# An attention and two-MLP kernel ordered by a list scheduler: the first batch's averages handed to the MLP inside SBUF, and the scheduler's costs rewritten

## The chip, the cores and the metric

The kernel runs on one core of a Trainium2 chip. The metric is the device time of one execution in microseconds (us). Before the change three runs gave 923.7, 921.27 and 922.58; the median is 922.58.

## The reference

Causal attention with a bias from a cumulative sum, then two MLPs, all in fp32:

```python
B, H, S, D = 4, 8, 576, 64
scores = (q @ k.T) / 8
bias = -(cum[..., :, None] - cum[..., None, :])       # cum = cumsum(max(s, 0))
scores = where(causal, -1e9, scores + minimum(bias, 0))
attn = softmax(scores)
x = (attn @ v)            # to [2304 tokens, 512]
h = x @ w_in              # 512 -> 2048
x = (h * clip(h + 3, 0, 6) / 6) @ w_out               # 2048 -> 512
h = maximum(maximum(x @ w1, x @ w2), x @ w3)          # 512 -> 768
out = h @ w_out2          # 768 -> 512
```

Input weights come as 64-bit floats, and the kernel turns their bits into fp32 itself.

## The kernel before, in words

**Work.** Attention goes by batch b (0 to 3) and pair of heads p (0 to 3), two heads j each; a head has five chunks c of 128 queries, the last of 64. Below, (b,p,j) is a head and (b,p) a pair. Each chunk is a *slot* (`slot`): TensorE writes scores to `ps_s` (line 768; two cuts of 288 columns for the last chunk), VectorE adds the mask and takes the maximum (783), ScalarE takes the exponential into `e` (791), TensorE transposes to `pt` (813) and ScalarE drains that (354), from batch 1 on with VectorE's remainder (820). `average` multiplies with the values into `px` (844 for batch 0 in fp32; 852 for the others, high and low parts) and adds to the pair's tile `x32` (356, 354, 868). `finish` transposes the reciprocals of the sums to `pt_r` (908), multiplies `x32` with them (912), splits the result into `xs`, a rounded part (329 or 331) and a remainder on GpSimd (335), and stores it to DRAM, `x_d[b]` (one DMA of 576 KB for each pair). Then the pair is `stored`.

**Keys and queries.** `prepare` loads a pair's q and k (`qb`, `kb`), splits them into a rounded part and a remainder, and joins them by SBUF-to-SBUF DMAs into `qt` and `kt`: for each head one small row from `cum_d`, two of `qt<-qb` and three of `kt<-kb`. A head's scores wait for all six. All DMAs are issued by one queue, SP's (line 308).

**First MLP.** A unit u is 288 tokens, half a batch. `load_xs` waits until a batch's four pairs are stored and loads them from `x_d` into a tile `x` of a stock of two (four DMAs of 288 KB for a unit). `hidden1` multiplies (`ps_h`, 433 to 435: three matmuls for each of four chunks), `gate` forms `gt`, and `reduce1` multiplies again (`ps_x`). The tokens go through 6 of 16 blocks of the hidden dimension in a first pass (z = 0) beside attention, and through the other 10 in a second pass (z = 1), for which `x` is loaded from `x_d` again. The second MLP (`ps_j`, `ps_o`) follows. Weights come in 512 KB pieces (`raw`, two buffers) and are turned into fp32 by `bits_in`: ScalarE 386, VectorE 388, 394, 399 and 404, then a cast 329 or 331 and a subtraction on GpSimd in two halves (335). `w_in` has its first six pieces, and `w_out` too, early in the program.

**Order.** Nothing is ordered by hand. Each of these functions is a Python generator that asks for an engine and a cost (`yield "DVE", dve2(512)`) or waits for an event, and `Flow` plays it as a list scheduler in time order: of the requests that wait on a free engine the one of lowest rank is taken, and the instruction is issued there and then. So the costs (`mm`, `dve1`, `dve2`, `act1`, `pool1`, `pool2`) and the landing time of a DMA (`Flow.landing`) decide the order in which every engine's queue is written, and on the chip each engine takes its queue strictly in that order. The first MLP's matmuls have a rank behind all attention, so they fill what attention leaves. Before the change a DMA's landing is counted as

```python
self.dma = max(self.dma, self.cur.t + 0.65) + nbytes / 360e3
ev.set(at=self.dma + 0.9)
```

and VectorE and GpSimd never hinder each other.

Of the kernel before, what the change touches and what calls it, by code (L numbers as in the profile page):

```python
# [9 lines left out]
F32 = mybir.dt.float32  # L10
# [12 lines left out]
P = 128  # L23
# [84 lines left out]


class Flow:  # L110
    LATENCY = {"PE": 0.2, "DVE": 0.13, "ACT": 0.15, "POOL": 0.08, "SP": 0.0}

    def __init__(self):
        self.agenda, self.n, self.now = [], 0, 0.0
        self.free = {e: 0.0 for e in self.LATENCY}
        self.ready = {e: [] for e in self.LATENCY}
        self.dma = 0.0
        self.cur = None
        self.live = set()
# [52 lines left out]
    def dispatch(self, engine):  # L172
        while self.ready[engine] and self.free[engine] <= self.now + 1e-9:
            _, _, th, cost, chained, taken = heapq.heappop(self.ready[engine])
            if taken:
                continue
            taken.append(engine)
            self.free[engine] = self.now + cost
            later = 0.0 if chained else self.LATENCY[engine]
            th.t = self.now + cost + later  # L180
            self.at(self.free[engine], lambda: self.dispatch(engine), ORDER)
            self.step(th, engine)

    def landing(self, nbytes):
        ev = Event(self)
        self.dma = max(self.dma, self.cur.t + 0.65) + nbytes / 360e3
        ev.set(at=self.dma + 0.9)
        return ev
# [29 lines left out]
def pool1(n):  # L218
    return 0.161 + n / 1200.0


def pool2(n):
    return 0.148 + n * 0.0021

# [32 lines left out]
def attn_moe_moe2(ctx, tc, q, k, v, s, w_in, w_out, w1, w2, w3, w_out2, out):  # L257
# [59 lines left out]

    COST = {
        "copy": {"POOL": pool1, "ACT": act1, "DVE": dve1},
        "sub": {"POOL": pool2, "DVE": dve2},  # L320
        "bank": {"ACT": act2, "DVE": dve2},
# [52 lines left out]
    def bits_in(src, out):  # L374
# [11 lines left out]
        act.activation(m, hi.bitcast(F32), AF.Square)  # L386
        yield "DVE", dve2(512)
        vec.scalar_tensor_tensor(
# [3 lines left out]
        top = m.bitcast(U32)  # L392
        yield "DVE", dve1(512)
# [4 lines left out]
        yield "DVE", dve2(512)  # L398
# [4 lines left out]
        yield "DVE", dve2(512)  # L403
        vec.scalar_tensor_tensor(
# [137 lines left out]
    def cumulate():  # L542
# [8 lines left out]
        yield flow.landing(4 * B * H * S)  # L551
        yield "DVE", dve1(S)
        vec.tensor_scalar(out=sp_t, in0=sp_t, scalar1=0.0, scalar2=None, op0=ALU.max)
        yield "DVE", dve2(S)
# [4 lines left out]
        yield "DVE", dve1(S)  # L559
        vec.tensor_scalar(  # L560
# [21 lines left out]
    def load(dst, src, nbytes):  # L582
        yield DMA
        copy(dst, src)
        return flow.landing(nbytes)
# [161 lines left out]
    def slot(i, item, tiny):  # L747
# [11 lines left out]
        for lo, hi in cuts:  # L759
            bank = yield S_.get()  # L760
            ps = make(bank, [P, 512], F32, "ps_s")
            o = ps[:, 0:hi - lo]
            if (b, p) == (0, 0):
                yield "PE", len(passes) * 4 * mm(hi - lo), False, i - AHEAD
# [45 lines left out]
        pt = make(bank, [P, c + 1, n], F32, "pt")  # L810
        yield "PE", 2 * mm(n) * (c + 1)
        for y in range(c + 1):
# [13 lines left out]
    def average(b, p, j, g):  # L826
# [12 lines left out]
        for x in range(nj):  # L839
            last = x == nj - 1  # L840
            z = max(0, x * P - o)
            if b == 0:
                yield "PE", 4 * mm(n - z), not last
                pe.matmul(
# [49 lines left out]
    def finish(b, p):  # L894
# [4 lines left out]
        for g in range(2):  # L899
            _, o, n = GROUP[g]  # L900
            bank = yield T.get()
            ps = make(bank, [P, 512], F32, "pt_r")
            yield "PE", 2 * mm(n)
            for c in ((0, 1), (4, 2, 3))[g]:
# [9 lines left out]
            )  # L914
            T.put(bank)
        si = yield XS.get()
        xs = make(si, [P, 2, S], F32R, "xs")
# [15 lines left out]
    x_over, mp_over, x_closed = event(), event(), event()  # L933

    def load_xs():
        for z in range(2):
            for u in range(NU):
                b, o = divmod(u, 2)
                yield stored[b, 0]
                xi = yield X.get()  # L940
# [142 lines left out]
    def combined(dst, a, b_, op, n):  # L1083
        yield "DVE", dve2(n)
        vec.tensor_tensor(out=dst, in0=a, in1=b_, op=op)
# [206 lines left out]
    def join(dst, a, b_, op):  # L1292
        yield "DVE", dve2(U1)
        vec.tensor_tensor(out=dst, in0=a, in1=b_, op=op)
# [383 lines left out]
```

## Time and profile before

| | |
|---|---|
| median of three runs | 922.58 us |
| the profiled execution | 921.71 us |
| its span, first to last instruction | 919.9 us |
| instructions | 18687 |
| TensorE (PE) busy | 893.6 us, 97% |
| VectorE (DVE) busy | 711.5 us, 77% |
| ScalarE (ACT) busy | 478.6 us, 52% |
| GpSimd (POOL) busy | 193.6 us, 21% |
| mean granted TensorE clock | 0.990 |

Busy time is a share of the whole span. A matmul's end is modelled and overlaps the next one, so a "busy" PE may still wait for pieces shorter than that. Times inside the trace count from the first instruction. PE is the matrix engine, PEld its weight loads, SPq the queue that issues the DMAs.

### The profile page before, as it was taken

How to read it: one execution, taken by the hardware profiler on the slowest of the kernel's cores; microseconds unless marked ns; L12 is line 12 of the kernel's file. 1: busy time of each engine (PE TensorE's matmuls, PEld its weight loads, DVE VectorE, ACT ScalarE, POOL GpSimd, SP SyncE). 2: the span in 40 equal slices, each digit the busy share in tenths (PEclk: the TensorE clock that was granted, in tenths of full speed). 3: DMA queues.
4: the chain of work that ended last, by engine and by line, in shares of the span. 5: the costliest groups of instructions: out<-in, count | busy, mean ns of one | idle time of the engine just before them, and what ended most of it. 6: DMA issues, size and time to landing. Idle time of an engine off the chain costs nothing.

```text
span 919.9 us, 18687 instructions
## 1 busy us (share of the span) xinstructions
PE 893.6 (97%) x6532; PEld 862.6 (94%) x6532; DVE 711.5 (77%) x1818; ACT 478.6 (52%) x1216; POOL 193.6 (21%) x242
## 2 busy tenths in 40 slices
PE   9887899999999999999999999999999999999998
PEld 6666799999999999999999999999999999999998
DVE  6877988887888449997785989985758576777994
ACT  5775677787777545564453455454213142323452
POOL 5557855556543123300000000000000000000000
PEclk9998799999999999999999999999999999999999
DMA  7999877787785147665566697938842121283542
GB/s 222 225 267 269 231 210 204 201 245 211 204 204 152 50 158 215 211 193 163 164 221 246 192 340 259 355 143 311 285 145 72 59 66 43 91 288 109 166 140 78
DMA packets 97269, 174.93 MB, mean 190 GB/s; under 512 B 10620, under 2 KB 59772, under 8 KB 97176
## 3 DMA queue, kind: packets, MB, share of 16 engines
q1 hardware_dynamic: 97176, 173.75, 61.7%
q8 instruction: 52, 0.85, 0.4%
q14 instruction: 41, 0.34, 0.1%
HBM read 97.99 MB, written 49.17 MB: 160 GB/s over the span
## 4 chain that ended last, share of the span: by engine, by line
PE 84%; DVE 7%; DMA 6%; issue 2%; ACT 1%; SPq 1%; POOL 0%; DVEq 0%; POOLq 0%; ACTq 0%
PE ps_j L433 7%; PE ps_j L434 7%; PE ps_j L435 7%; PE ps_x L433 7%; PE ps_h L433 7%; PE ps_x L435 7%; PE ps_x L434 6%; PE ps_h L434 6%; PE ps_h L435 6%; PE ps_s L768 6%; PE px L852 4%; PE pt L813 4%; PE ps_o L434 2%; PE ps_o L435 2%; PE ps_o L433 2%
## 5 line engine op out<-in xcount | busy, mean ns | idle before, releaser
L433 PE MATMUL ps_h<-x,w 128*128 128x288 f32 x512 | 155.2, 303 | 0.0
L433 PE MATMUL ps_x<-gt,w 128*128 128x288 f32 x512 | 152.8, 298 | 0.3 <-DVE g L981 0.3
L435 PE MATMUL ps_x<-gt,w 128*128 128x288 f32 x512 | 151.1, 295 | 0.0
L434 PE MATMUL ps_h<-x,w 128*128 128x288 f32 x512 | 151.1, 295 | 0.0
L434 PE MATMUL ps_x<-gt,w 128*128 128x288 f32 x512 | 150.5, 294 | 0.3 <-DVE gt L335 0.3
L435 PE MATMUL ps_h<-x,w 128*128 128x288 f32 x512 | 150.7, 294 | 0.0
L434 PE MATMUL ps_j<-xf,wf 128*128 128x288 f32 x432 | 127.9, 296 | 0.0
L433 PE MATMUL ps_j<-xf,wf 128*128 128x288 f32 x432 | 127.7, 296 | 0.0
L435 PE MATMUL ps_j<-xf,wf 128*128 128x288 f32 x432 | 127.5, 295 | 0.0
L977 ACT ACTIVATE u<-ps_h,half 128x288 f32<-128x288 f32 x128 | 63.9, 499 | 97.8 <-PE ps_h L435 97.4
L791 ACT ACTIVATE e<-e,tiny 128x128 f32<-128x128 f32 (+4 forms) x160 | 95.9, 600 | 30.5 <-DVE tiny L783 29.6
L768 PE MATMUL ps_s<-kt,qt 128*128 128x288 f32 (+9 forms) x384 | 96.9, 349 | 8.7 <-DMA kt<-kb 4.3
L433 PEld LDWEIGHTS ps_h<-x,w 128*128 128x128 f32 x512 | 96.4, 188 | 1.0 <-DVE g L981 0.2
L433 PEld LDWEIGHTS ps_x<-gt,w 128*128 128x128 f32 x512 | 96.2, 188 | 0.9 <-DVE g L981 0.5
L434 PEld LDWEIGHTS ps_x<-gt,w 128*128 128x128 f32 x512 | 96.2, 188 | 0.8 <-DVE gt L335 0.6
L434 PEld LDWEIGHTS ps_h<-x,w 128*128 128x128 f32 x512 | 96.4, 188 | 0.1
L435 PEld LDWEIGHTS ps_h<-x,w 128*128 128x128 f32 x512 | 96.2, 188 | 0.0
L435 PEld LDWEIGHTS ps_x<-gt,w 128*128 128x128 f32 x512 | 96.2, 188 | 0.0
L783 DVE CUSTOM_DVE_ANT_0 e<-ps_s,above 128x128 f32<-128x128 f32 (+4 forms) x160 | 75.7, 478 | 21.5 <-PE ps_s L768 19.9
L981 DVE SCALAR_TENSOR_TENSOR g<-u,ps_h 128x288 f32<-128x288 f32 x128 | 57.6, 450 | 41.0 <-ACT u L977 39.9
L329 ACT ACTIVATE gt<-g 128x288 fp32r<-128x288 f32 x128 | 56.5, 441 | 50.0 <-DVE g L981 49.6
L434 PEld LDWEIGHTS ps_j<-xf,wf 128*128 128x128 f32 x432 | 81.4, 188 | 0.0
(157 smaller groups left out, 2112.7 us busy)
## 6 DMA issues: line engine op xcount, KB each, us to landing
x<-x_d SPq DMA_DIRECT2D x64, 288.0 KB
f_d<-wf SPq DMA_DIRECT2D x30, 512.0 KB
wf<-f_d SPq DMA_DIRECT2D x30, 512.0 KB
kt<-kb SPq DMA_DIRECT2D x90, 144.0 KB
raw<-in_w_out_dram SPq DMA_DIRECT2D x22, 512.0 KB
x_d<-xs SPq DMA_DIRECT2D x16, 576.0 KB
raw<-in_w_dram SPq DMA_DIRECT2D x18, 512.0 KB
qt<-qb SPq DMA_DIRECT2D x30, 288.0 KB
```

Source lines behind the costliest of these rows:

```text
L329: act.activation(dst, src, AF.Copy)
L433: pe.matmul(ps, lhsT=wh, rhs=xh, start=first, stop=False, skip_group_check=again)
L434: pe.matmul(ps, lhsT=wh, rhs=xl, start=False, stop=False, skip_group_check=again)
L435: pe.matmul(ps, lhsT=wl, rhs=xh, start=False, stop=last, skip_group_check=again)
L768: pe.matmul(o, lhsT=lhs[:, qs], rhs=rhs[:, lo:hi], start=(x == 0), stop=(x == len(passes) - 1),)
L783: vec.tensor_tensor_reduce(out=e[:, lo:hi], in0=ps[:, 0:hi - lo], in1=above[:, shift + lo:shift + hi], scale=-0.125, scalar=m0, op0=ALU.ad ...
L791: act.activation(e[:, :w], e[:, :w], AF.Exp, bias=m0, scale=-1.0, accum_out=r,)
L813: pe.transpose(pt[:, y, :], e[P - n:, y * P:(y + 1) * P], ident[P - n:, P - n:])
L852: pe.matmul(px[:, z:n], lhsT=vhl[:, x, j].rearrange("p l d -> p (l d)"), rhs=src[:, hl, x, z:n], start=(x + hl == 0), stop=(last and hl == 1),
L977: act.activation(ut, ps, AF.Relu, bias=half, scale=1.0 / 6.0)
L981: vec.scalar_tensor_tensor(out=g, in0=ut, scalar=1.0, in1=ps, op0=ALU.min, op1=ALU.mult)
```

## The change

Two things are done at once.

1. `finish` for batch 0 no longer uses `xs`. It takes both `x` tiles of the first MLP when pair (0,0) ends, and writes each pair's rounded part and remainder straight into them, by halves of 288 columns. After the fourth pair a unit's `x_ready` is set, and `load_xs` has nothing to load for units 0 and 1 in the first pass. The halves are still stored to `x_d` for the second pass, as eight DMAs of 288 KB out of `x`.
2. `Flow` counts otherwise. A matmul costs n/2245 + 0.004 (an fp32 one, all passes, n/600 + 0.01, a transpose n/1200 + 0.003). A DMA is counted by the length of its contiguous pieces, and slower from SBUF to SBUF. A cost of class `Held` (the GpSimd ones and VectorE's with operands in SBUF) takes a port that VectorE and GpSimd share, and starts only when that is free.

```diff
     def dispatch(self, engine):
...
+                if isinstance(one[3], Held) and self.port > self.now + 1e-9:
+                    passed.append(one)
+                else:
+                    chosen = one
...
     def landing(self, nbytes):
         ev = Event(self)
-        self.dma = max(self.dma, self.cur.t + 0.65) + nbytes / 360e3
-        ev.set(at=self.dma + 0.9)
+        took, after = self.moved
+        self.dma = max(self.dma, self.cur.t) + took
+        ev.set(at=self.dma + after)
         return ev
...
 def mm(n):
-    return n / 2400.0 + 0.003
+    return n / 2245.0 + 0.004
...
 def pool2(n):
-    return 0.148 + n * 0.0021
+    return Held(0.148 + n * 0.0021)
+def held2(n):
+    return Held(dve2(n))
...
     def copy(dst, src):
+        rows, r = src.ap[0][1], 4 if src.dtype != I64 else 8
+        nbytes = r
+        for _, n in src.ap:
+            nbytes *= n
+        r *= min(run_of(src), run_of(dst))
+        sides = [a.space == DRAM for a in (src, dst)]
+        if rows > 1:
+            r = min(r, nbytes // rows)
+        one = 0.010 if r <= 64 else 0.008 + r * 37.5e-6
+        if not any(sides):
+            one *= 1.6 if r < 3000 else 1.95
+        flow.moved = max(1.0, nbytes / r / 16.0) * one * 1.25, 1.5 if sides[0] else 0.9 if sides[1] else 1.0
...
     def finish(b, p):
...
+        if b == 0:
+            if p == 0:
+                for u in range(2):
+                    item = yield X.get()
+                    first_x[u].set((make(item, [P, 2, KD, U1], F32R, "x"), item))
+            for u in range(2):
+                x, item = yield first_x[u]
+                xc = x32[:, u * U1:(u + 1) * U1]
+                yield from rounded(x[:, 0, p], xc, U1, ON["xh"])
+                yield from minus(x[:, 1, p], xc, x[:, 0, p].bitcast(F32), U1, ON["xl"])
+                first_count[u] += 1
+                if first_count[u] == NPAIR:
+                    x_ready[0, u].set((x, item))
+            X32.put(xi)
+            for u in range(2):
+                x, item = yield first_x[u]
+                d = yield from load(
+                    x_d[0][:, p, :, u * U1:(u + 1) * U1].rearrange("l p t -> p l t"),
+                    x[:, :, p], 8 * P * U1,
+                )
+            yield d
+            stored[0, p].set()
+            finished[0] += 1
+            return
...
     def load_xs():
...
+                if (z, b) == (0, 0):
+                    yield x_ready[z, u]
+                    continue
```

Because of the second part the order changes on every engine, and three places show it. Line numbers after the change are 59 higher in this part of the code (768 is 827, 813 is 872, 844 is 903, 852 is 911, 908 is 967, 783 is 842, 912 is 971).

PE before, where pair (0,3) ends. `vhl` marks averages of batch 1:

```order
L768 MATMUL ps_s<-kt,qt 128x256 x2
L908 MATMUL pt_r<-ident,ex 128x128 x2
L813 MATMUL pt<-ident,e_188 128x64 x5
L813 MATMUL pt<-ident,e 128x128
L768 MATMUL ps_s<-kt,qt 128x384 x2
L908 MATMUL pt_r<-ident,ex 128x128 x3
L813 MATMUL pt<-ident,e 128x128 x2
L852 MATMUL px<-e_1185,vhl 128x320 x2
```

PE after, the same place, up to the first `ps_h` (492):

```order
L903 MATMUL px<-e2p,vf_745 128x320 x3
L903 MATMUL px<-e2p,vf_745 128x192
L903 MATMUL px<-e2p,vf_745 128x64
L967 MATMUL pt_r<-ident,ex 128x128 x5
L827 MATMUL ps_s<-kt,qt 128x128 x2
L827 MATMUL ps_s<-kt,qt 128x256 x2
L872 MATMUL pt<-ident,e 128x128
L827 MATMUL ps_s<-kt,qt 128x384 x2
L872 MATMUL pt<-ident,e 128x128 x2
L492 MATMUL ps_h<-x,w 128x288
```

Before, 70 PE instructions lie between the last `pt_r` of pair (0,3) and the first `ps_h`; now 9 do. Ahead of the first `ps_h` stood 130 `ps_s`, 160 `pt` and 84 `px`; now 96, 123 and 56. The 99 that went are batch 1's and come behind it; in front of it, batch 0's last three heads now have PE to themselves, one after the other.

SP before, the store of pair (0,3) and what follows up to the last loads of unit 0 and the first of unit 1:

```order
L308 DMA x_d_58<-xs 128x2x576
L308 DMA qt<-qb 64x1152
L308 DMA kt<-kb 64x576
L308 DMA x<-x_d_58 128x2x288
L308 DMA kt<-cum_d 2x576
L308 DMA qt<-qb 64x576
L308 DMA kt<-kb 64x576 x2
L308 DMA qt<-qb 64x1152
L308 DMA kt<-kb 64x576
L308 DMA x<-x_d_58 128x2x288 x4
```

All eight loads `x<-x_d` of units 0 and 1 are gone after the change.

SP after, where the last head of batch 0, (0,3,1), is joined:

```order
L367 DMA kt<-cum_d 2x576
L367 DMA vf<-in_v_dram 128x640
L367 DMA qt<-qb 64x576
L367 DMA kt<-kb 64x576
L367 DMA x_d_58<-x 128x2x288
L367 DMA kt<-kb 64x576
L367 DMA x_d_58<-x 128x2x288
L367 DMA qt<-qb 64x1152
L367 DMA kt<-kb 64x576
L367 DMA raw<-in_w_out_dram 128x512 x2
L367 DMA x_d_58<-x 128x2x288 x2
```

The two single stores are pair (0,1)'s. The store of that pair came six rows behind the last join of (0,3,1) before; now it stands among these joins. The sizes of all DMAs up to that last join add up to 15.2 MB before and 15.0 MB after, in 66 and 67 DMAs.

DVE after, behind the last maximum of (0,3,1), from the third instruction to the last multiplication of batch 0 (`dm`, `da` and `w` turn a piece of `w_out` into fp32, `x_905` is the pair's `x32`):

```order
L453 TENSOR_SCALAR da<-dm 128x512
L939 TENSOR_SCALAR sums<-sums 128x10
L458 SCALAR_TENSOR_TENSOR da<-dm,da 128x512
L941 RECIPROCAL sums<-sums 128x10
L463 SCALAR_TENSOR_TENSOR da<-raw,da 128x512
L447 SCALAR_TENSOR_TENSOR dm<-dm,raw 128x512
L390 CAST w<-da 128x512
L453 TENSOR_SCALAR da<-dm 128x512
L458 SCALAR_TENSOR_TENSOR da<-dm,da 128x512
L971 TENSOR_TENSOR x_905<-x_905,pt_r 128x256
L463 SCALAR_TENSOR_TENSOR da<-raw,da 128x512
L971 TENSOR_TENSOR x_905<-x_905,pt_r 128x320
```

With a `dm` (447) and a copy of `px` (415) ahead of these, fourteen instructions lie between the last maximum and the end of the pair. Before, batch 1's maxima and remainders stood in this stretch as well; they have moved behind it.

## Rows read from the trace of the kernel before

**Rows 1.** Stretches: length, busy us (instructions) by engine, granted clock, DMA share, GB/s.

```profile
0.00:113.00 113.00, 93.73 (x508) 73.98 (x509) 89.55 (x245) 73.44 (x198) 71.60 (x91) 0.92 0.92 244
113.00:460.00 347.00, 345.01 (x2611) 335.40 (x2611) 272.67 (x727) 225.63 (x575) 121.97 (x152) 1.00 0.65 185
460.00:920.00 460.00, 454.89 (x3416) 453.18 (x3415) 349.29 (x849) 179.48 (x444) 0.00 (x0) 1.00 0.53 180
```

**Rows 2.** Timeline of PE: start, length, what, [idle before, who ended it].

```profile
66.93 0.71 PE L768 MATMUL ps_s<-kt,qt 128*128 128x128 f32 x4 [0.95 <-DMA kt<-kb]
...
80.99 0.52 PE L813 MATMUL pt<-ident,e 64*128 64x64 f32 x5 [2.90 <-ACT e L791]
83.11 1.65 PE L844 MATMUL px<-e1p,vf 128*128 128x256 f32 x4 [1.59 <-DVE x L356]
...
113.01 0.34 PE L433 MATMUL ps_h<-x,w 128*128 128x288 f32 x1
```

**Rows 3.** Shorter stretches, columns as in rows 1.

```profile
23.00:46.00 23.00, 18.74 (x113) 14.27 (x112) 20.53 (x50) 16.57 (x44) 13.59 (x16) 1.00 1.00 225
46.00:69.00 23.00, 18.87 (x119) 15.47 (x119) 16.69 (x58) 17.27 (x50) 11.84 (x16) 1.00 1.03 267
...
161.00:184.00 23.00, 23.00 (x175) 21.93 (x174) 18.51 (x58) 17.27 (x51) 13.07 (x18) 1.00 0.76 201
```

**Rows 4.** Timeline of SP, the queue that issues the DMAs.

```profile
13.73 5.08 SPq L308 DMA_DIRECT2D raw<-in_w_in_dram  x2
...
60.43 0.60 SPq L308 DMA_DIRECT2D kt<-kb  x1
...
66.18 0.53 SPq L308 DMA_DIRECT2D x_d<-xs  x1
...
102.49 0.53 SPq L308 DMA_DIRECT2D x_d<-xs  x1
...
112.20 3.18 SPq L308 DMA_DIRECT2D x<-x_d  x4
```

**Rows 5.** Timeline, the end of pair (0,3).

```profile
96.27 0.49 DVE L912 TENSOR_TENSOR x<-x,pt_r 128x320 f32<-128x320 f32 x1
96.97 0.67 ACT L329 ACTIVATE xs<-x 128x576 fp32r<-128x576 f32 x1
...
100.27 1.25 POOL L335 TENSOR_TENSOR xs<-x,xs 128x288 fp32r<-128x288 f32 x1
```

**Rows 6.** The chain that ended last, 60 to 114 us: start, length, what.

```profile
71.08 8.43 DMA raw<-in_w_out_dram
79.52 0.67 ACT dm L386
```

**Rows 7.** Groups of the page: busy us, mean ns | idle before.

```profile
L783 DVE CUSTOM_DVE_ANT_0 e<-ps_s,above 128x128 f32<-128x128 f32 (+4 forms) x160 | 75.7, 478 | 21.5 <-PE ps_s L768 19.9
```

**Rows 8.** Groups of DVE in 0 to 113 us, by form.

```profile
L404 DVE SCALAR_TENSOR_TENSOR da<-raw,da 128x512 uint32<-128x512 uint32 x11 | 10.3, 936 | 0.1
L388 DVE SCALAR_TENSOR_TENSOR dm<-dm,raw 128x512 f32<-128x512 f32 x12 | 10.1, 838 | 4.7 <-ACT dm L386 4.7
L399 DVE SCALAR_TENSOR_TENSOR da<-dm,da 128x512 uint32<-128x512 uint32 x11 | 9.8, 891 | 0.2
...
L394 DVE TENSOR_SCALAR da<-dm 128x512 uint32<-128x512 uint32 x11 | 5.6, 513 | 0.1
```

**Rows 9.** The same for POOL.

```profile
L335 POOL TENSOR_TENSOR xs<-x,xs 128x288 fp32r<-128x288 f32 x8 | 7.3, 916 | 0.8 <-DVE xs L331 0.4 <-DVE sums L880 0.4
```

**Rows 10.** Timeline of POOL, pair (0,1)'s last remainder.

```profile
63.17 0.99 POOL L335 TENSOR_TENSOR xs<-x,xs 128x288 fp32r<-128x288 f32 x1
```

**Rows 11.** Stretches, columns as in rows 1.

```profile
78.00:82.00 4.00, 0.62 (x6) 0.39 (x5) 1.79 (x5) 1.93 (x5) 4.00 (x6) 1.00 1.07 294
82.00:86.00 4.00, 2.89 (x10) 2.71 (x11) 3.93 (x7) 2.15 (x6) 4.00 (x5) 0.55 1.06 237
86.00:90.00 4.00, 4.00 (x13) 2.84 (x12) 2.87 (x11) 1.97 (x5) 2.18 (x3) 0.60 1.01 339
```

More of the change, by code (lines that the diff above doesn't have):

```diff
@@ L107, in rank @@
         return self.prio
+class Held(float):
+    pass
 class Flow:
@@ L117, in __init__ @@
         self.dma = 0.0
+        self.port = 0.0
         self.cur = None
@@ L172, in dispatch @@
     def dispatch(self, engine):
[L173 to L176, printed above, removed]
+        ready = self.ready[engine]
+        while ready and self.free[engine] <= self.now + 1e-9:
+            passed, chosen = [], None
+            while ready and chosen is None:
+                one = heapq.heappop(ready)
+                if one[5]:
+                    continue
[3 more added lines that the diff above has]
+                    chosen = one
+            for one in passed:
+                heapq.heappush(ready, one)
+            if chosen is None:
+                return
+            _, _, th, cost, chained, taken = chosen
             taken.append(engine)
             self.free[engine] = self.now + cost
+            if isinstance(cost, Held):
+                self.port = self.now + cost
+                for other in ("DVE", "POOL"):
+                    if other != engine:
+                        self.at(self.port, lambda other=other: self.dispatch(other), ORDER)
             later = 0.0 if chained else self.LATENCY[engine]
@@ L198, in mm, with mm4, mmt @@
 def mm(n):
-    return n / 2400.0 + 0.003
+    return n / 2245.0 + 0.004
+def mm4(n):
+    return n / 600.0 + 0.01
+def mmt(n):
+    return n / 1200.0 + 0.003
 def dve1(n):
@@ L218, in pool1, with held1 @@
 def pool1(n):
-    return 0.161 + n / 1200.0
+    return Held(0.161 + n / 1200.0)
 def pool2(n):
-    return 0.148 + n * 0.0021
+    return Held(0.148 + n * 0.0021)
+def held1(n):
+    return Held(dve1(n))
+def held2(n):
+    return Held(dve2(n))
 DMA = ("SP", 0.45)
@@ L305, in stack, with run_of @@
         return [(pl, f"{tag}{x}") for x in range(n)]
-    def copy(dst, src):
+    def run_of(a):
+        r = 1
+        for step, n in reversed(a.ap):
+            if step != r:
+                break
+            r *= n
+        return r
+    def copy(dst, src):
+        rows, r = src.ap[0][1], 4 if src.dtype != I64 else 8
[10 more added lines that the diff above has]
+        flow.moved = max(1.0, nbytes / r / 16.0) * one * 1.25, 1.5 if sides[0] else 0.9 if sides[1] else 1.0
         sp.dma_start(
@@ L318, in attn_moe_moe2 @@
     COST = {
-        "copy": {"POOL": pool1, "ACT": act1, "DVE": dve1},
-        "sub": {"POOL": pool2, "DVE": dve2},
+        "copy": {"POOL": pool1, "ACT": act1, "DVE": held1},
+        "sub": {"POOL": pool2, "DVE": held2},
         "bank": {"ACT": act2, "DVE": dve2},
@@ L386, in bits_in @@
         act.activation(m, hi.bitcast(F32), AF.Square)
-        yield "DVE", dve2(512)
+        yield "DVE", held2(512)
         vec.scalar_tensor_tensor(
@@ L392, in bits_in @@
         top = m.bitcast(U32)
-        yield "DVE", dve1(512)
+        yield "DVE", held1(512)
         vec.tensor_scalar(
@@ L397, in bits_in @@
         )
-        yield "DVE", dve2(512)
+        yield "DVE", held2(512)
         vec.scalar_tensor_tensor(
@@ L402, in bits_in @@
         )
-        yield "DVE", dve2(512)
+        yield "DVE", held2(512)
         vec.scalar_tensor_tensor(
@@ L551, in cumulate @@
         yield flow.landing(4 * B * H * S)
-        yield "DVE", dve1(S)
+        yield "DVE", held1(S)
         vec.tensor_scalar(out=sp_t, in0=sp_t, scalar1=0.0, scalar2=None, op0=ALU.max)
-        yield "DVE", dve2(S)
+        yield "DVE", held2(S)
         vec.tensor_tensor_scan(
@@ L558, in cumulate @@
         QHL.put(a)
-        yield "DVE", dve1(S)
+        yield "DVE", held1(S)
         vec.tensor_scalar(
@@ L763, in slot @@
             if (b, p) == (0, 0):
-                yield "PE", len(passes) * 4 * mm(hi - lo), False, i - AHEAD
+                yield "PE", len(passes) * mm4(hi - lo), False, i - AHEAD
             else:
@@ L810, in slot @@
         pt = make(bank, [P, c + 1, n], F32, "pt")
-        yield "PE", 2 * mm(n) * (c + 1)
+        yield "PE", mmt(n) * (c + 1)
         for y in range(c + 1):
@@ L842, in average @@
             if b == 0:
-                yield "PE", 4 * mm(n - z), not last
+                yield "PE", mm4(n - z), not last
                 pe.matmul(
@@ L902, in finish @@
             ps = make(bank, [P, 512], F32, "pt_r")
-            yield "PE", 2 * mm(n)
+            yield "PE", mmt(n)
             for c in ((0, 1), (4, 2, 3))[g]:
@@ L915, in finish @@
             T.put(bank)
+        if b == 0:
[21 more added lines that the diff above has]
+            finished[0] += 1
+            return
         si = yield XS.get()
@@ L933, in attn_moe_moe2 @@
     x_over, mp_over, x_closed = event(), event(), event()
+    first_x, first_count = [event(), event()], [0, 0]
     def load_xs():
@@ L938, in load_xs @@
                 b, o = divmod(u, 2)
+                if (z, b) == (0, 0):
+                    yield x_ready[z, u]
+                    continue
                 yield stored[b, 0]
@@ L1083, in combined @@
     def combined(dst, a, b_, op, n):
-        yield "DVE", dve2(n)
+        yield "DVE", held2(n)
         vec.tensor_tensor(out=dst, in0=a, in1=b_, op=op)
@@ L1292, in join @@
     def join(dst, a, b_, op):
-        yield "DVE", dve2(U1)
+        yield "DVE", held2(U1)
         vec.tensor_tensor(out=dst, in0=a, in1=b_, op=op)
```

## The prediction, as it was put on record

> **What bounds the kernel now.** I read the busy time by stretches first. From 113 us on, PE is busy 345.01 of 347.00 us and then 454.89 of 460.00; in the first 113 us only 93.73 of 113.00, at a mean granted clock of 0.92 [rows 1]. So behind 113 us the kernel is bound by PE's work, and what can be won there is the 7 us of idle time. Ahead of it some 20 us are idle, and part of the rest runs at the lower clock. 113 us is no chance place: it is when the first `ps_h` starts [rows 2], the MLP's matmul that fills what attention leaves open. Since all PE work behind it lies almost without a gap, the time of the kernel is the moment of the first `ps_h` plus the PE work that the order puts behind it. The prediction is these two numbers.
>
> The shorter stretches tell what bounds the part ahead. From 23 to 69 us the DMA share is 1.00 and 1.03 while PE is busy 18.7 of 23 us [rows 3]: the joins of keys and queries are late. In PE's timeline the scores of the last head of batch 0, (0,3,1), start at 66.93, ended by DMA `kt<-kb` [rows 2]. Its own last join was issued at 60.43 [rows 4], 6.5 us earlier. From there to the first `ps_h` 46 us pass, and two things fill them. First, the pair ends late: `x32` is multiplied last at 96.27 [rows 5], after waits of PE of 2.90 us for the exponential and 1.59 us for a copy [rows 2]. The chain of waits puts these down to a piece of `w_out` that was on its way for 8.43 us, from 71.08, and to the decoding behind it [rows 6]: ScalarE and VectorE stood in their queues at a piece that the scheduler had thought landed. Second, the trip through DRAM: the remainder ends at 101.5 [rows 5], the store is issued at 102.49, the last loads of the unit at 112.20 [rows 4], and the matmul starts at 113.01. From the last multiplication that is 16.3 us.
>
> **The change, part by part.** *The trip through DRAM* goes: unit 0 is ready when the last remainder is written. Eight loads of 288 KB leave SP's queue; four stores of 576 KB become eight of 288 KB, off the path, since only the second pass reads them. Four casts of 576 columns become eight of 288: one of 576 took 0.67 [rows 5], so less than 0.67 more for each pair beside other work; I cost it at nothing but for the last one, which is on the path.
>
> *The order.* 99 PE instructions of batch 1 move behind the first `ps_h`. In a dense stretch of attention and MLP together 175 instructions take 23.00 us [rows 3], 0.131 each, so the work behind grows by 99 x 0.131 = 13.0 us. The part behind was 919.9 - 113.0 = 806.9 us, and becomes 819.9. This is what the change has to pay: if the first `ps_h` came no earlier than 100.0, nothing would be won.
>
> *When the first `ps_h` comes.* The DMAs up to the last join of (0,3,1) are 15.0 MB where they were 15.2. While the DMA engines are full that is the same moment, so the scores of that head start at 66.9 again. From there I add up the path by the new order, in which PE and VectorE do little but this head:
>
> - the first scores 0.71 [rows 2], six maxima at 0.478 each [rows 7], 2.9: 70.5;
> - the fourteen instructions of VectorE up to the last multiplication. Eight are the decoding: two each of 0.838, 0.513, 0.891 and 0.936 [rows 8], 6.4. The other six (a copy, two on the sums, a cast, two multiplications) at the 0.49 of the multiplication [rows 5], 2.9. Together 9.3: 79.8;
> - the cast, at most 0.67 [rows 5], and GpSimd's remainder, 0.92 [rows 9]: 81.4.
>
> Exponentials, transposes and averages of that head run on other engines beside these fourteen. If the decoding were not there they would be the path, so it is no sum of both.
>
> Two things may delay this. The stores of pair (0,1) now stand among the joins of (0,3,1), and SP waits for what it is to store: behind them in SP's queue are the last `qt` and `kt` of that head, and PE's scores wait for those. Before, the last remainder of that pair ended at 63.17 + 0.99 = 64.2 [rows 10] and the store was issued at 66.18 [rows 4]; were it as late now, the joins would move by 66.2 - 60.4 = 5.8 us. At best they move by nothing, since 12 fewer score instructions stand ahead of that pair's end. And the granted clock may fall: in 82 to 90 us, behind a stretch in which PE was busy 0.62 of 4 us, it was 0.55 and 0.60 [rows 11], where about half of the 6.9 busy us, 3.4, was lost. So between 0 and 9.2 us; I take 3.6, nearer to the low end, because part of a late join is covered (its DMAs then find the engines less full) and because the old stall of PE had a cause that the new order takes away. On the other side, SP stood 5.08 us at two pieces of `w_in` at 13.73 [rows 4]; one of them is issued later now, and if the joins come earlier by the 4 us or so of that wait, the path ends at 77.4.
>
> So the first `ps_h` comes at 85.0 (77.4 to 90.6). Sum: 819.9 + 85.0 = 904.9 us of span. The profiled execution is 921.71 for a span of 919.9, and the median of the runs 922.58, so 2.7 go on top: **907.6 us** (900 to 913 for this case alone).
>
> *Behind the first `ps_h`* I change nothing. The filler must last: units 0 and 1 have 288 matmuls in the first pass, 288 x 0.131 = 37.7 us, and the order spreads them to beyond the end of batch 1 as before. In the second pass and the second MLP PE's order is nearly the same. VectorE's and ScalarE's shares of casts change hands there; that work lies beside 450 of 460 us of PE.
>
> *The costs themselves* are no instructions; their whole effect is the order.
>
> **Rivals.** *The end of batch 0 stays where it was* (no change). VectorE is busy 89.55 of 113 us [rows 1], and if it and the DMAs, not the order, set the pair's end, the multiplication ends at 96.27 + 0.49 again; with 0.67 and 0.92 the first `ps_h` comes at 98.4, and the time is 819.9 + 98.4 + 2.7 = 921.0. The 16.3 us of the trip are then nearly all paid back by the work that moved. For it speaks that the order still puts two decodings into the tail, whose pieces may land late. Against it: VectorE has nine maxima, with their reads, and all of batch 1's remainders less to do ahead of that point.
>
> *The clock falls for the last heads* (slower). From (0,2,1) on each head of batch 0 now has PE alone, in the order score, transpose, average, with nothing of batch 1 between; 121 PE instructions lie from there to the first `ps_h`. In 46 to 69 us 119 took 18.87 us at full clock [rows 3]; at half, 121 would take 19.2 more. With none of it hidden the first `ps_h` comes at 104.2, and the time is 926.8. It decides once 17.7 of the 19.2 us are lost. Against it: the clock held at 1.00 through 23 to 69 us though PE was idle for a fifth of it [rows 3]. The Trainium skill's page "TensorE: Matmul & The Clock Gate" (Part 1) speaks for it: it calls the half rate the default, released only by activity. By that rule a thinner stretch of PE is the place to lose the clock, and the time would be this rival's; the trace agrees in the stretch behind 78 us and not in the one before.
>
> **How the numbers follow.** About 0.3%, 2.8 us, is what a measurement of this kernel can tell from no change: faster is below 919.8, slower above 925.3. The forecast has 0.79; the end of batch 0 unmoved 0.13, which counts as the same; the clock 0.08, slower. The range holds the forecast's own bounds, with 1 us below for joins that come earlier still, and reaches up to the first rival: 899 to 921. It leaves out the clock and a little of either side.
>
> **What would show it.** The first `ps_h` at 77 to 91 us; no `x<-x_d` for units 0 and 1; the first scores of (0,3,1) near 67 us, without a piece of `w_out` holding ScalarE for several us behind them; PE dense from the first `ps_h` on. Wrong would be: the first `ps_h` at 96 or later; a clock near 0.5 between 60 us and it; SP standing at a store `x_d<-x` ahead of the last joins by more than 6 us; or new gaps of PE behind it, where batch 1's scores wait for their joins or unit 2 for its loads, each of which adds its own length.

## The result, and the profile after

The changed kernel takes 913.19 us (median; 912.86 to 913.57) against 923.14 for the kernel before in the same session: ratio 0.9888, 95% interval 0.9874 to 0.9901. The profiled execution has a span of 911.8 us, 8.1 less than before. The forecast was 907.6, so two thirds of the forecast gain of 15 us came; the result lies inside the range of 899 to 921.

The three stretches of [rows 1], of the kernel after (columns as there):

```profile
0.00:113.00 113.00, 101.40 (x608) 81.60 (x609) 86.96 (x256) 78.67 (x213) 63.72 (x86) 0.98 0.86 225
113.00:460.00 347.00, 342.63 (x2559) 331.25 (x2559) 273.82 (x728) 225.60 (x577) 127.35 (x160) 0.99 0.67 188
460.00:912.00 452.00, 447.58 (x3369) 446.81 (x3367) 342.10 (x836) 174.22 (x430) 0.00 (x0) 1.00 0.54 181
```

By 113 us PE has done 608 instructions where it had done 508: a lead of 100. The next 347 us hold only 2559 where they held 2611: 52 of the 100 are lost again. Shorter stretches show where:

```profile
92.00:115.00 23.00, 22.03 (x166) 20.63 (x166) 21.51 (x61) 18.41 (x52) 17.04 (x21) 1.00 0.79 186
115.00:138.00 23.00, 19.55 (x123) 16.94 (x123) 20.29 (x58) 14.14 (x39) 17.20 (x22) 0.90 0.82 205
138.00:161.00 23.00, 23.00 (x167) 21.93 (x167) 17.54 (x60) 16.66 (x48) 12.92 (x18) 0.95 0.65 181
```

From 115 to 138 us PE does 123 instructions, 52 fewer than in a dense stretch [rows 3]. PE's timeline has the last head of batch 0, the first `ps_h` and the new gap:

```profile
69.44 2.38 PE L903 MATMUL px<-e2p,vf 128*128 128x320 f32 x10 [0.53 <-ACT e2p L413]
71.62 1.06 PE L827 MATMUL ps_s<-kt,qt 128*128 128x128 f32 x6
...
78.69 4.06 PE L903 MATMUL px<-e2p,vf 128*128 128x320 f32 x10 [0.53 <-ACT e2p L413]
82.59 0.72 PE L967 MATMUL pt_r<-ident,ex 128*128 128x128 f32 x5
...
86.04 0.38 PE L492 MATMUL ps_h<-x,w 128*128 128x288 f32 x1
...
123.47 0.29 PE L494 MATMUL ps_x<-gt,w 128*128 128x288 f32 x1
...
124.26 0.29 PE L494 MATMUL ps_h<-x,w 128*128 128x288 f32 x1
...
138.94 0.49 PE L492 MATMUL ps_x<-gt,w 128*128 128x288 f32 x1
```

The end of the pair, which answers to [rows 5], takes 1.6 us where the trip through DRAM took 16.3:

```profile
83.01 0.42 DVE L971 TENSOR_TENSOR x<-x,pt_r 128x256 f32<-128x256 f32 x1 [1.17 <-PE pt_r L967]
...
83.95 0.48 DVE L971 TENSOR_TENSOR x<-x,pt_r 128x320 f32<-128x320 f32 x1
...
84.47 0.44 ACT L388 ACTIVATE x<-x 128x288 fp32r<-128x288 f32 x1 [1.25 <-DVE x L971]
...
84.99 1.00 POOL L394 TENSOR_TENSOR x<-x,x 128x288 fp32r<-128x288 f32 x1 [2.56 <-ACT x L388]
```

The first `ps_h` starts at 86.04. Between 123.47 and 138.94 there is no `ps_x`, and behind the one at 124.26 no `ps_h` either: all nine `gt` tiles are full, and the next `ps_x` needs the sixth piece of `w_out`. Its decoding lies thinly in VectorE's queue, and ends with GpSimd's subtraction:

```profile
124.26 0.77 DVE L447 SCALAR_TENSOR_TENSOR dm<-dm,raw 128x512 f32<-128x512 f32 x1
...
127.48 0.63 DVE L453 TENSOR_SCALAR da<-dm 128x512 uint32<-128x512 uint32 x1
...
132.93 0.99 DVE L458 SCALAR_TENSOR_TENSOR da<-dm,da 128x512 uint32<-128x512 uint32 x1
...
134.05 0.68 DVE L463 SCALAR_TENSOR_TENSOR da<-raw,da 128x512 uint32<-128x512 uint32 x1
...
135.79 0.41 DVE L390 CAST w<-da 128x512 fp32r<-128x512 f32 x1
...
138.27 0.72 POOL L394 TENSOR_TENSOR w<-da,w 128x256 fp32r<-128x256 f32 x1
```

Before, that subtraction stood at 120.81:

```profile
120.81 0.95 POOL L335 TENSOR_TENSOR w<-da,w 128x256 fp32r<-128x256 f32 x1
```

**An account of PE's time.** For every kind and shape of PE instruction I took the lower quartile of the time from its start to the next start (median over the kernels) as its dense pace, and call what a kernel takes beyond that its *loss*. All fourteen kernels run the same 6532 PE instructions, so span minus loss is the same in all by construction (845.2 to 845.7 us): the table tells where time is lost, not why. It is of one execution each, and executions of one kernel differ: the changed kernel's by 0.7 us, those of the kernel before lay between 917.65 and 928.88, and e4's profiled one, at 930.59, is among its slowest. So a difference of a microsecond or two in a cell says little. In us, by stretch; "first" and "145th" are `ps_h`, the 145th being the first of batch 1; "left" is how many of the first pass's 864 matmuls are not yet done when attention's last `pt_r` starts. The names are those of the experiments below.

```
          0-84 84-113 113-140 140-230 230-345 345-460 460-end  loss  span  first 145th last pt_r left
before    27.5  13.8    3.0     8.2     9.0     2.4    10.4    74.3 919.9 113.0 193.9  326.8   192
after     25.9   2.7   10.6     8.5     8.2     2.0     8.5    66.4 911.8  86.0 197.2  321.1   192
e1        25.0  10.5    6.3     8.9    10.7    15.8     9.7    86.9 932.2  94.9 195.1  345.0    54
e2        24.9  18.0    7.8     8.6     8.7     1.9     9.1    79.0 924.2 126.7 213.9  324.5   258
e3        25.6   5.4    2.4    13.7     9.9    16.5    11.1    84.6 930.3  87.0 199.7  340.5    54
e4        28.3   7.1    8.0    11.8     9.1     6.3    13.0    83.6 928.8 100.7 195.1  338.8   123
e6        25.0   8.0    2.7    14.0     8.3     8.4    10.9    77.3 922.6  89.1 202.1  323.3   192
e7        23.3  11.8    7.2     8.8     9.2     3.5    11.8    75.6 920.9  92.3 195.5  327.7   177
e8        24.2   8.7    4.1     9.9     7.9     1.9     9.1    65.8 911.1  84.3 201.2  314.5   234
e9        24.2   4.3    9.3     8.4     8.0     2.5     8.9    65.6 910.9  84.4 195.5  310.9   255
e10       26.1   3.2    2.6    12.7     7.8     4.0     8.9    65.3 910.6  86.3 202.5  316.4   201
e11       24.7   4.6    9.1     9.4     7.7     1.9     8.9    66.3 911.6  87.6 200.5  314.5   240
e12       25.5   5.1    9.9    10.2     7.6     3.4    13.0    74.7 920.1  88.9 206.3  323.7   192
e13       24.2   8.7    4.1     8.0     8.3     4.8     8.9    67.0 912.5  84.3 194.2  317.4   201
```

So of the 12.7 us that the change gains up to 113 us it gives 7.6 back by 140, and it gains another 1.9 behind 460.

### The profile page after: what moved, and what is told of

It is laid out like the page before. It is cut to its first block, busy times and chain, and to the rows that moved or that the text cites. A ratio compares the mean times of both kernels' runs of the same rounds, so it can differ in the third digit from the quotient of the medians.

```text
span 911.8 us, 18686 instructions
## 1 busy us (share of the span) xinstructions
PE 891.6 (98%) x6532; PEld 859.7 (94%) x6532; DVE 702.9 (77%) x1817; ACT 478.5 (52%) x1218; POOL 191.1 (21%) x245
## 4 chain that ended last, share of the span: by engine, by line
PE 84%; DVE 8%; DMA 3%; ACT 3%; issue 1%; POOL 1%; SPq 0%; POOLq 0%; DVEq 0%; ACTq 0%
PE ps_j L493 7%; PE ps_j L494 7%; PE ps_j L492 7%; PE ps_s L827 6%; PE ps_h L492 6%; PE ps_x L492 6%; PE ps_x L494 6%; PE ps_x L493 6%; PE ps_h L493 6%; PE ps_h L494 6%; PE pt L872 5%; PE px L911 4%; PE ps_o L493 2%; PE ps_o L494 2%; PE ps_o L492 2%; DMA raw<-in_w_dram 2%
## 5 line engine op out<-in xcount | busy, mean ns | idle before, releaser
L850 ACT ACTIVATE e<-e,tiny 128x128 f32<-128x128 f32 (+4 forms) x160 | 95.9, 600 | 28.2 <-DVE tiny L842 27.2
L494 PEld LDWEIGHTS ps_x<-gt,w 128*128 128x128 f32 x512 | 96.3, 188 | 0.1
L827 PE MATMUL ps_s<-kt,qt 128*128 128x288 f32 (+9 forms) x384 | 92.3, 342 | 1.2 <-DVE tiny L842 1.2
L493 PEld LDWEIGHTS ps_j<-xf,wf 128*128 128x128 f32 x432 | 81.4, 188 | 0.0
```

Source lines behind the costliest of these rows:

```text
L493: pe.matmul(ps, lhsT=wh, rhs=xl, start=False, stop=False, skip_group_check=again)
L494: pe.matmul(ps, lhsT=wl, rhs=xh, start=False, stop=last, skip_group_check=again)
L827: pe.matmul(o, lhsT=lhs[:, qs], rhs=rhs[:, lo:hi], start=(x == 0), stop=(x == len(passes) - 1),)
L850: act.activation(e[:, :w], e[:, :w], AF.Exp, bias=m0, scale=-1.0, accum_out=r,)
```

## The experiments

### One half of the change at a time: e1 and e2

e1 is the kernel before with `finish`'s new branch and the skip in `load_xs`, and the old counts. e2 is the changed kernel without these two.

```diff
+        if b == 0:
...
+            for u in range(2):
+                x, item = yield first_x[u]
...
+                if (z, b) == (0, 0):
+                    yield x_ready[z, u]
+                    continue
```

> The kernel before with the hand-over inside SBUF alone; the scheduler's costs are the old ones. Theory A (both parts count: the hand-over cuts the trip, the new costs cut the end of batch 0): pair (0,3) still ends near 96 us, the first ps_h comes near 99, and since 62 PE instructions fewer than before stand ahead of it (8.1 us more behind it) the time is about 806.9 + 8.1 + 99 + 2.7 = 917, some 6 us below before. Theory B (the new costs did it all): within 2 us of before. Theory C (the hand-over did it all): about 913, as the change.

> The change without the hand-over: the new costs alone, batch 0 through xs, x_d and the loads again. Theory A: pair (0,3) ends near 83 us as in the change, the first ps_h near 100 to 105, with batch 1's attention in between as the only work of PE; 914 to 919. Theory B: 913, as the change. Theory C: 923, as before.

Measured: e1 936.56 us, ratio 1.0132 (1.0105 to 1.0159); e2 926.36, ratio 1.0023 (1.0012 to 1.0035). Neither half makes the kernel faster; together they do. Both miss what was expected. The table says where. In e2 batch 0 ends early (last `pt_r` at 85.9), but its `x` still goes through DRAM: the last load of unit 0 is issued at 108.85, and the first `ps_h` stands 17.8 us behind it in PE's order, at 126.7, where it stood 5.0 behind it before. PE is thin till then:

```profile
92.00:115.00 23.00, 16.32 (x70) 14.50 (x71) 16.40 (x41) 10.98 (x29) 16.86 (x21) 0.58 0.85 226
```

e1 brings the first `ps_h` to 94.9 and has lost 41.8 us by 140 us, 2.5 less than before (44.3). But its attention ends at 345.0, and PE then starves: 15.8 us of loss at 345 to 460. Its stretches, the first just ahead of that end and the second behind it:

```profile
330.00:345.00 15.00, 13.94 (x105) 13.26 (x104) 4.41 (x9) 5.38 (x14) 2.40 (x3) 1.00 0.06 21
345.00:360.00 15.00, 12.23 (x93) 12.00 (x91) 1.75 (x4) 3.38 (x7) 1.57 (x2) 1.00 0.55 189
```

VectorE is nearly idle there: the second pass's weights are loaded and decoded only when attention is done, and only 54 matmuls of the first pass are left to cover it.

### One count at a time: e3 and e4

e3 is the changed kernel with `Held` costs as plain numbers (no shared port); e4 has the old landing of a DMA.

```diff
-class Held(float):
-    pass
+def Held(x):
+    return x
```

```diff
-        took, after = self.moved
-        self.dma = max(self.dma, self.cur.t) + took
-        ev.set(at=self.dma + after)
+        self.dma = max(self.dma, self.cur.t + 0.65) + nbytes / 360e3
+        ev.set(at=self.dma + 0.9)
```

> The change, with the shared port of VectorE and GpSimd not counted in the scheduler (all other new costs kept). If counting the port helps, it is slower than the change by 1 us or more; if it only makes the scheduler put off the decoding of the last w_out piece (that piece's decoding is asked for earlier in this order: the sixteenth ps_x stands at PE place 604, not 647), PE's thin stretch at 116 to 140 us shrinks, and it is faster by 2 to 5 us.

> The change, with the old landing time of DMAs in the scheduler (all other new costs kept). If the DMA count is what freed the end of batch 0, pair (0,3) ends at 90 us or later again, behind waits for DMAs, and the time is 917 to 921. If not, 913.

Measured: e3 932.36, ratio 1.0100 (1.0071 to 1.0128); e4 928.05, ratio 1.0038 (1.0016 to 1.0061). In e4 batch 0's last `pt_r` comes at 96.3 again (95.9 before, 83.0 after), and PE waits for joins, `ps_s` for `kt<-kb`, for 5.5 us of 50 to 110, 4.8 of them at once: beside the other new counts it is the count of DMAs that brings the end of batch 0 forward (e1, with all the old counts, has it at 90.8). Its time lies above the 917 to 921 expected; part of that may be a late tail like e3's, since its attention ends at 338.8. e3 keeps the early first `ps_h` and even has no thin stretch at 113 to 140. It loses elsewhere (e3: 115 to 138, 184 to 207, 340 to 460):

```profile
115.00:138.00 23.00, 22.93 (x175) 21.63 (x173) 19.37 (x65) 17.88 (x54) 11.46 (x16) 1.00 0.92 217
184.00:207.00 23.00, 21.29 (x138) 19.08 (x136) 16.41 (x51) 15.16 (x42) 10.82 (x14) 0.85 0.91 244
340.00:460.00 120.00, 111.65 (x796) 108.75 (x797) 90.16 (x185) 58.77 (x122) 13.15 (x14) 0.97 0.56 181
```

Two suspicions follow. *Tail*: e1 and e3 end attention late, with 54 matmuls left, since the averages of the last two heads have ranks (first slot of the head + 10 or 12, so 160 to 167) not ahead of the MLP's 159 and 160, so the scheduler may put the MLP ahead of them. *Stock*: what e3 does not lose at 113 to 140 it loses at 184 to 207.

### The tail first: e6, e7 and e9

The averages' ranks are capped, in e3 (e6), in e1 (e7) and in the changed kernel (e9).

```diff
-                flow.start(i + BEHIND, reciprocals(b, p))
+                flow.start(min(i + BEHIND, 158), reciprocals(b, p))
...
-                    flow.start(i + BEHIND + 2 * g, average(b, p, j, g))
+                    flow.start(min(i + BEHIND + 2 * g, 158), average(b, p, j, g))
```

> e3 (the changed kernel without the shared port) with the ranks of the averages capped at 158, ahead of the first MLP's 159 and 160, so that the last pair's averages are not put behind the MLP. In the written order the last pt_r then stands behind 378 ps_h and 294 ps_x (e3: 432 and 378). Theory A (what e3 lost, it lost because its MLP work was used up before attention ended, and PE then starved until the second pass's weights were decoded): attention ends near 320 us in place of 340.5, the thin stretch 345 to 460 goes (14 us), and the time is 912 to 918. Rival B (the order without the port is slower everywhere, the late end is a symptom): the lost time turns up elsewhere, 926 or more.

> e1 (the hand-over alone, old costs) with the same cap. Last pt_r behind 390 ps_h and 297 ps_x (e1: 432 and 378). Theory A: attention ends near 325 in place of 345.0, the starving stretch behind it (some 13 us more than before's) goes, time 919 to 924: the hand-over alone is then worth about what it frees ahead of the first ps_h less what is lost at 92 to 126, 0 to 4 us against before. Rival B: 932 or more, as e1.

> The changed kernel with the cap alone. Last pt_r behind 330 ps_h and 279 ps_x (369 and 303 without). Theory A (there is hardly anything to starve for behind attention in the changed kernel): attention ends near 313, nothing else moves, 911 to 914. Rival: with more MLP work left for the stretch where the second pass's weights are decoded it gains another 2 to 3 us, 909 to 911.

Measured: e6 923.28, ratio 1.0002 (0.9979 to 1.0026); e7 921.63, ratio 0.9976 (0.9952 to 1.0001); e9 913.15, ratio 0.9889 (0.9859 to 0.9918). e1 gains 15 us by the cap, e3 9, the changed kernel nothing though its attention ends 10 us sooner. e7, 340 to 460:

```profile
340.00:460.00 120.00, 119.14 (x898) 118.53 (x897) 101.31 (x206) 64.08 (x136) 15.54 (x15) 1.00 0.58 184
```

So the starving tail is what had hidden the hand-over's own worth: with the cap it is 0 to 4 us, and its interval touches no change. The kernel before with the cap alone was not run. For e6 theory A held by half: the late end went, but 8.4 us of loss stay at 345 to 460, with as many matmuls left as before and after. Why the order without the port still starves there is open.

### Decode `w_out` sooner: e8

```diff
-WO_PRIO, WO_STEP = 50, 3
+WO_PRIO, WO_STEP = 40, 3
```

> The changed kernel with the cap and with WO_PRIO 40 in place of 50, so that the six early w_out pieces are decoded sooner: in the written order the 16th ps_x stands at place 598 of PE in place of 647, and the last pt_r of pair 5 behind 48 ps_x in place of 15. To be set beside e9 (cap alone). Theory A (PE ran thin at 113 to 140 us since the sixth w_out piece was late): the stretch fills, the first 145 ps_h come some 4 us sooner in lost time, 906 to 910. Rival B (the filler of batch 0 is a fixed stock of 144 ps_h and 144 ps_x, and what is spent sooner is missing later, as e3 showed at 197 to 204): the thin stretch moves to 185 to 205, time within 2 us of e9's. Rival C (VectorE is full there and decoding sooner puts attention off as much): as B, with pair 5 later.

Measured: 913.00, ratio 0.9894 (0.9869 to 0.9920): e9's time. The thin stretch left 113 to 140 (9.3 us of loss became 4.1) and came back at 84 to 113 (4.3 became 8.7) and 140 to 230 (8.4 became 9.9). In the first of these PE stood 1.65 us at an average that waited for VectorE, and the granted clock fell to 0.57 for 100 to 108 us. There the stock of MLP work was far from used up (222 of 288 matmuls left at 113 us). Both rivals to A are left: VectorE full (C), or a fixed stock of MLP work (B).

### Less work for VectorE: e10 and e11

```diff
+        if short:
+            RAW.put(r)
+            return m, am
         top = m.bitcast(U32)
...
-        wf, am = yield from bits_in(src, None)
+        wf, am = yield from bits_in(src, None, key[0] == "o" and key[1] in (3, 4, 5))
```

and, in e11 alone,

```diff
-    ("wh", False): DVE,
+    ("wh", False): DVE + ACT,
```

> e9 (the changed kernel with the averages' ranks capped) with three of VectorE's five steps left out of the decoding of the w_out pieces 3 to 5 (the two that build da and the one that joins the low bits): nine instructions, by the means of the changed kernel's rows (0.49, 0.94 and 0.84 us) 6.8 us of VectorE taken out of the stretch 84 to 140, and the sixth piece is ready sooner. The weights of these pieces are then not the reference's. Theory C (VectorE is what this stretch lacks: e8 only moved the thin stretch from 113-140 to 92-113): the loss there falls by 4 to 7 us, time 906 to 910. Rival B (a fixed stock of MLP work, spent sooner and missing at 185 to 205 instead): 912 to 914.

> e9 with the cast of the early weights given to VectorE or ScalarE, whichever the scheduler finds free, in place of VectorE alone. Theory C: VectorE gets up to 12 casts of 0.48 us off its queue, some of them in 84 to 140 us: 908 to 912. Rival: the first ps_h stands some 13 instructions later on PE and ScalarE's exponentials are put off; 913 to 917.

Measured: e10 912.23, ratio 0.9881 (0.9855 to 0.9906); e11 913.55, ratio 0.9895 (0.9869 to 0.9920). e11 took casts off VectorE too, but its losses are e9's, with the first `ps_h` 3.2 us later. e10 speaks for B: the 906 to 910 of C did not come. With some 6.8 us of VectorE's work gone PE is dense from 92 to 138, 351 instructions where e9 had 289, and then lacks work where B put it. Of the 7.8 us of loss that leave 84 to 140 (against e9) 4.3 come back at 140 to 230; the others are at 345 to 460 (1.5) and ahead of 84 (1.9). e10, three stretches:

```profile
92.00:115.00 23.00, 23.00 (x178) 21.91 (x177) 20.10 (x62) 18.83 (x54) 17.38 (x22) 1.00 0.76 181
115.00:138.00 23.00, 23.00 (x173) 21.81 (x173) 19.59 (x62) 17.10 (x52) 15.14 (x20) 1.00 0.86 222
184.00:207.00 23.00, 21.14 (x150) 18.08 (x149) 19.45 (x64) 17.97 (x53) 12.85 (x17) 1.00 0.92 246
```

The last matmul of batch 0's units is done at 186.1 and the first of batch 1's comes at 202.46:

```profile
186.11 0.29 PE L497 MATMUL ps_x<-gt,w 128*128 128x288 f32 x1
187.92 0.76 PE L875 MATMUL pt<-ident,e 64*128 64x64 f32 x6 [0.69 <-DVE e L882]
189.81 0.55 PE L970 MATMUL pt_r<-ident,ex 128*128 128x128 f32 x3 [0.60 <-DVE e L882]
...
202.46 0.38 PE L495 MATMUL ps_h<-x,w 128*128 128x288 f32 x1
```

### The old counts of matmuls: e12

e9 with `mm` as before, four of them for an fp32 matmul and two for a transpose.

> e9 with the old costs of matmuls and transposes (n/2400 + 0.003, four and two of them) and everything else of the change: what that part of the counts is worth. By the written order the first ps_h stands 19 instructions later, ps_x 16 at 658 in place of 647. Theory A (this part is minor, since the old costs are within a tenth of the new): 913 to 916, with the thin stretch at 113 to 140 as before. Rival (each count is needed): 920 or more, as without the port (e6).

Measured: 923.10, ratio 0.9989 (0.9974 to 1.0004). The rival was right: numbers within a tenth of each other are worth 10 us of order. Against e9 the loss is spread: 0.6 to 1.8 us in each stretch up to 230, and 4.1 behind 460.

### Refill the stock sooner: e13

```diff
+                if z == 0:
+                    d = event()
+                    d.set(at=flow.cur.t + 3)
                 yield d
                 x_ready[z, u].set((x, xi))
```

> e8 (the changed kernel, averages' ranks capped, w_out decoded sooner) where the scheduler counts a unit's x as there 3 us after its last load is issued, in place of its own count of the landing. In e8 the 144th ps_h started at 162.4 us, the last ps_x of batch 0's stock at 193.0, and the 145th ps_h only at 201.2, though the last of unit 2's loads was issued at 190.2. In the new order the 145th ps_h stands 41 places earlier on PE (1080 in place of 1121). Theory B (a fixed stock of MLP work has to last until the next batch's x is there, so only refilling it sooner helps): the 145th ps_h starts near 196, the loss of some 2.5 us over the dense pace at 170 to 230 goes, time 909.5 to 911.5. Rival D (PE's gaps at 184 to 207 do not come from the empty stock): 912.5 to 914.

Measured: 914.69 (913.87 to 916.01), ratio 0.9903 (0.9884 to 0.9922): no gain, and above both forecasts. The mechanism came as expected: the 145th `ps_h` at 194.2, and the loss at 140 to 230 down by 1.9 us. The time did not: at 345 to 460 the loss rose from 1.9 to 4.8. The same 60 us of e8 and of e13:

```profile
400.00:460.00 60.00, 60.00 (x456) 60.00 (x455) 48.63 (x111) 27.90 (x60) 0.00 (x0) 1.00 0.53 174
```

```profile
400.00:460.00 60.00, 57.98 (x433) 57.15 (x433) 48.70 (x110) 26.43 (x58) 0.00 (x0) 1.00 0.53 169
```

MLP work that runs sooner is missing behind attention: 234 matmuls were left in e8, 201 in e13, where the second pass's weights are being decoded. But the number left alone does not set that loss: before and after have 192 and lose 2.4 and 2.0.

## Why the prediction was right, and where it was off

**The sum.** Span = moment of the first `ps_h` + what lies behind it: 86.04 + 825.8 = 911.8, forecast 85.0 + 819.9 = 904.9. This holds by definition; right or wrong are its terms.

**The first `ps_h`** came at 86.04 for 85.0 (77.4 to 90.6): right. Its parts were less so. "The scores of that head start at 66.9 again", because the joins would set it, failed: they start at 71.62. The last join of (0,3,1) is issued at 60.83, 0.4 later than before [rows 4], but in the new order these scores stand behind all averages of the head before it, and start when the last of those does. The 3.6 us that I had put on the stores and the clock happened to cover most of the 4.7. From there the path was 14.4 us long for a forecast 14.5 (66.9 to 81.4), but not by the forecast's parts, so this too is in part luck. VectorE had done what stands ahead of the first multiplication at 81.84, sooner than I had summed, and then stood 1.17 us for `pt_r`: the averages, which I had put beside the path, ended it. The clock did fall, to 0.50 from 78.75 to 82.17: the ten averages of (0,3,1) took 4.06 us where the same ten of (0,3,0) took 2.38. That is 1.7 us on PE, of which at most VectorE's 1.17 reached the first `ps_h`; the rival had 19.2. One reading was wrong without changing the sum: the loads at 112.20 [rows 4] are unit 1's, and the last of unit 0 was issued at 107.98.

**The moved work** was forecast at 13.0 us. The part behind was 806.9 us with 33.2 of loss, 773.7 dense; it is 825.8 with 40.5, 785.3 dense. So the 99 instructions weigh 11.6 us.

**The step that failed** is "*Behind the first `ps_h`* I change nothing. The filler must last ... and the order spreads them to beyond the end of batch 1 as before." The loss behind the first `ps_h` grew by 40.5 - 33.2 = 7.3 us, which is the whole miss: +1.0 for the first `ps_h`, -1.4 for the moved work, +7.3, together 6.9 of span. It is the sum of +2.6 (86 to 113), +7.6 (113 to 140), 0.4 more between 140 and 580, and -3.3 behind 580, where the new order is better than I had said.

**What stands in its place.** The order did spread the filler to beyond the end of batch 1, as I had said: the last `ps_x` of units 0 and 1 starts at 236.6 (239.5 before), and 18 of their 288 matmuls are left when batch 1's first `ps_h` starts. But the filler was held up on the way. The sixth piece of `w_out` was ready at 121.8 us before, 29 us ahead of the first `ps_x` that needed it; now it is ready at 139.0, and the `ps_x` ahead of that one was done at 123.8. The forecast moved the start of the filler forward by 27 us and did not ask when the weights that it needs would be there; in the new order the last of them comes 17 us later.

That explains the place, 113 to 140, and not the whole loss: in e3, e7, e8 and e10 the piece comes sooner, and the loss turns up elsewhere. In all eleven profiles in which the first `ps_h` comes at 84 to 95 us, and in e4 (100.7), the loss from there to 230 us is 18 to 24 us; it is 11.3 before (113.0) and 10.3 in e2 (126.7). A second limit is the stock: the 288 matmuls of units 0 and 1 last 37.7 us by the pace of [rows 3], they had to last from 113.0 to 193.9, and now from 86.0 to 197.2. In e3, e8 and e10 the last of them starts at 187.8, 193.0 and 186.1, 8 to 16 us before the first of batch 1. The stock does not account for what e8 loses at 84 to 113, nor for e7, where 15 are left and no piece is late. Why the loss is so much the same whatever the order stays open.

The end of that stretch lies still for a reason that the forecast did not hold either. Batch 1's attention ends sooner than before (last `pt_r` at 175.7 for 180.9), and the last load of its first unit is issued sooner, but its first `ps_h` comes later. Before, and after:

```profile
190.33 0.54 SPq L308 DMA_DIRECT2D x<-x_d  x1
...
193.87 0.30 PE L433 MATMUL ps_h<-x,w 128*128 128x288 f32 x1
```

```profile
187.63 0.62 SPq L367 DMA_DIRECT2D x<-x_d  x1
...
197.19 0.38 PE L492 MATMUL ps_h<-x,w 128*128 128x288 f32 x1
```

From that load to that matmul it is 2.5 to 4.2 us in the four kernels with the old count of DMAs (before, e1, e4, e7), 9.2 to 15.1 in the nine with the new one, and 4.0 in e13, which overrides it there. PE has no idle time just ahead of either, so the written order sets it: the count that brings batch 0's end forward puts batch 1's start back. Yet e13, which mends this on top of e8, gains no time.

**The rivals.** *The end of batch 0 stays* fell: its last `pt_r` came 12.9 us sooner, and without the count of DMAs it does not (e4). *The clock falls for the last heads* had the right place and a tenth of the price. The Trainium skill, "TensorE: Matmul & The Clock Gate" (Part 1), which calls the half rate the default that activity releases, was right of the new thin stretch too: the granted clock is 0.90 at 115 to 138, after PE had worked thinly from 124 on. It was 0.50, the lower level of 1.2 GHz, from 133.4 to 140.2; PE was busy for 6.0 us of that, so by estimate up to 3 of the 10.6 us lost at 113 to 140 could be the clock's. Whether they are was not tried.

**"The costs themselves are no instructions; their whole effect is the order"** is true, and I had given that effect no term outside batch 0. It is as large as the hand-over: each of the three counts taken back makes the kernel some 10 us slower or more (e6, e12 against e9; e4), and the hand-over taken back 13 (e2). All four are within 0.4% of the kernel before: the gain belongs to all parts together, and cannot be divided among them. Whether the new counts gain because they are nearer to the chip, or because this one order happens to be a good one, is not shown either: no run changes a count by as much in another direction, and e4 was not run with the cap.

## What to carry to other kernels

When work that fills another stage's gaps is made ready sooner, ask what else it needs on the way, and when the next portion of it comes: if a weight that it needs is ready later, or that moment stays, part of the gain comes back as a gap further on. Count a lead by stretches of the profile until it is either in the end time or lost. And a list scheduler's counts are part of a kernel like its instructions: try each edit of the code again under the order that it will run in, since e1 lost 15 us (e7) by ranks that its edit had not touched.

## What the runs showed of the hardware

Most of VectorE's instructions with all operands in SBUF took longer while GpSimd worked (not the short reciprocal: 0.210 and 0.204 us in the trace of before); those that read PSUM did not. In the changed kernel's trace the same step with GpSimd idle and with GpSimd working beside it, and what GpSimd did (the last row):

```profile
78.02 0.69 DVE L458 SCALAR_TENSOR_TENSOR da<-dm,da 128x512 uint32<-128x512 uint32 x1
...
80.75 1.09 DVE L458 SCALAR_TENSOR_TENSOR da<-dm,da 128x512 uint32<-128x512 uint32 x1
```

```profile
80.46 1.97 POOL L394 TENSOR_TENSOR w<-da,w 128x256 fp32r<-128x256 f32 x2 [8.00 <-DVE w L390]
```

In the trace of before, up to 460 us, the remainder `gt` on VectorE takes 0.454 us where GpSimd does not overlap it (24 of them) and 0.883 where it does for more than 60% of the time (5); the remainder `e<-pt,e` of 512 columns, which reads PSUM, takes 0.686 and 0.683. The Trainium skill, "SBUF — State Buffer" ("Who interferes with whom"), calls the pair of ports that the two engines share an exclusive lock, and says that a VectorE instruction with two SBUF inputs contends with a GpSimd instruction that reads SBUF. The rows agree: the step that reads `dm` and `da` takes 0.40 us longer beside two GpSimd subtractions of 1.97 us together. That the scheduler counts this is worth 10 us here (e6 against e9), by the order alone.
